# Two reloads moved into a static instruction order, a longer TensorE warm-up, and a new order table

## The chip, the core and the metric

One NeuronCore of a Trainium2 chip runs one program. Its engines each follow an instruction list of their own: PE (TensorE, matrix products), ACT (ScalarE), DVE (VectorE), POOL (GpSimd) and SP (SyncE, which here issues DMA transfers). They meet through semaphores. The metric is the device time of one execution in microseconds (us), and lower is better.

## What is computed

Three stages are chained, all in fp32, the outputs of one being the inputs of the next: landmark attention, a gated MLP, and an MLP with the Mish function.

```python
# q, k, v: (4, 8, 576, 64); m = 32 landmarks
q_lm = q.reshape(B, H, m, S // m, D).mean(axis=3)
k_lm = k.reshape(B, H, m, S // m, D).mean(axis=3)
A, Bm, C = sm(q, k_lm), sm(q_lm, k_lm), sm(q_lm, k)
Z = Bm.transpose(0, 1, 3, 2) / (norm1(Bm) * norminf(Bm) + 1e-06)
for _ in range(6):
    Z = 2 * Z - Z @ Bm @ Z
x = (A @ Z @ C @ v)                # to (2304, 512)
x = (x @ w1) * (x @ w2) @ w3 @ w_out          # 512 -> 1024 -> 1024 -> 512
h = x @ w_in                                  # 512 -> 2048
return (h * np.tanh(softplus(h))) @ w_out2    # 2048 -> 512
```

## The kernel before, in words

**Weights arrive as 64-bit words** and are decoded on the chip, piece by piece, into fp32. A piece `u` takes five steps: `ld u` is the load (SP), `da u` takes the top bits (`top_bits`, L234 on ACT or L236 on DVE), `dm u` the sign (`sign`, L241 on ACT or L243 on DVE), `ds u` rescales (`rescale`, L246, ACT alone) and `db u` joins the halves (`join`, L250, DVE alone). Pieces are named `wo0` to `wo7` (w_out of the gated MLP), `w30` to `w315` (w3), `w000` and up (w1 and w2), and plain numbers (the Mish MLP's w_in and w_out). The raw words lie in a pool of four slots (`raw`) and one of three (`raw2`, tile `raw_74`); a slot is given back when the last step that reads it is issued.

**Matrix products.** w3 and w_out of the gated MLP are multiplied first, in steps `mm n x` (L390, in fp32, each step two matmuls of 128x512). Attention's products of k and q with the landmark means are L564, L485 and L647; the means come from the reductions at L443 (DVE), and copies into block-diagonal tiles at L466 (ACT) and L468 (POOL). The later products are done in three matmuls each, of operands that are split into a high and a low part (`mm3`, L222 to L224): the high part is a copy on ACT (L254), the low part a subtraction on DVE (L259).

**The Mish MLP** goes over three token tiles of 768, and in each over eight quarters of w_in; `g` counts the quarters through all tiles, 0 to 7 in the first, 8 to 15 in the second. A quarter takes seven products by a Strassen scheme, `Z0 g` to `Z6 g` (42 matmuls 128x384), with sums `S`, `Q`, `R`, `C12`, `C21`, `C22` of their results (L1345, DVE, or L1364, ACT), Mish in `E1` to `E3` (L1341 and L1342, ACT), low parts `L1` to `L3` (DVE), and the output products `O0 g` to `O3 g` (36 matmuls 128x512 in all), which run one quarter behind. For a new token tile the tokens' operands are summed and split: `yt`, `yh` (ACT) and `yl` (DVE). While the first tile runs, each split quarter of w_in is stored to DRAM (`zd q`), and each split piece of w_out too (`ws f`), for the later tiles to read back: quarters lie in the two buffers `zw` and `hs`, pieces of w_out in the slots `W_65`, `W_66`, `wy`, `ym` and others.

**What sets the order.** Attention, the gated MLP and the first token tile are cut into named steps. `ORDER` (L29) is one string of step names in a fixed sequence, with an engine behind `@` where a step may run on either of two. `issue()` (L314) walks it and emits each step's instructions, so that an engine's program is the sequence of its own steps in the string. In front of that stand `SPIN` warm-up matmuls on a tile of ones (L1434). Behind it the second and third tile are written out in a loop over `g`; `reload(g)` (L1441) issues the read of the quarter after next and of two pieces of w_out.

```python
    def reload(g):
        if NQ <= g + 2 < NG:
            nc.sync.dma_start(out=f32(zw_all(g)), in_=zd[(g + 2) % NQ])
        for u in (2 * g + 5, 2 * g + 6):
            if 2 * NQ <= u < 2 * NG:
                wo_load(u)

    for g in range(5, NQ):
        reload(g)
    for g in range(NQ, NG):
        ...
```

SP takes its transfers in program order: one whose semaphores are not yet there holds all behind it.

Of the kernel before, what the change touches and what calls it, by code (L numbers as in the profile page):

```python
# [19 lines left out]
SPIN = 20  # L20
# [161 lines left out]
def kernel(  # L182
# [14 lines left out]
    nc = tc.nc  # L197
# [1247 lines left out]
            if 2 * NQ <= u < 2 * NG:  # L1445
                wo_load(u)

    for g in range(5, NQ):
        reload(g)
# [59 lines left out]
```

## Time and profile before

| what | value |
|---|---|
| median of 3 runs | 748.26 us (747.41 to 748.49) |
| the profiled execution | 748.68 us, span 746.9 us |
| busy PE, DVE, ACT, POOL | 720.5, 429.6, 421.0, 16.8 us |
| share of the span | 96%, 58%, 56%, 2% |
| granted TensorE clock, mean | 0.988 of full speed |
| DMA | 141.48 MB, mean 189 GB/s |

The span runs from the profile's first instruction to its last; the time of the execution is a little longer. A clock of 1.00 is 2.4 GHz and 0.50 is 1.2 GHz, the two levels that TensorE's clock has; a value between them is a mean over a stretch.

### The profile page before, as it was taken

How to read it: one execution, taken by the hardware profiler on the slowest of the kernel's cores; microseconds unless marked ns; L12 is line 12 of the kernel's file. 1: busy time of each engine (PE TensorE's matmuls, PEld its weight loads, DVE VectorE, ACT ScalarE, POOL GpSimd, SP SyncE). 2: the span in 40 equal slices, each digit the busy share in tenths (PEclk: the TensorE clock that was granted, in tenths of full speed). 3: DMA queues.
4: the chain of work that ended last, by engine and by line, in shares of the span. 5: the costliest groups of instructions: out<-in, count | busy, mean ns of one | idle time of the engine just before them, and what ended most of it. 6: DMA issues, size and time to landing. Idle time of an engine off the chain costs nothing.

```text
span 746.9 us, 14026 instructions
## 1 busy us (share of the span) xinstructions
PE 720.5 (96%) x5652; PEld 616.6 (83%) x5652; DVE 429.6 (58%) x909; ACT 421.0 (56%) x835; POOL 16.8 (2%) x37
## 2 busy tenths in 40 slices
PE   4999999999999999999999999799999999999997
PEld 1445547888999999999898899688988899889986
DVE  4888768878656746777676777433323463232232
ACT  5897877787858777775665765332222342222222
POOL 0011100100000000000000000000000000000000
PEclk8999999999999999999999999899999999999999
DMA  8877574444325255337456646956445555455502
GB/s 330 295 247 242 172 213 165 122 127 129 117 82 166 90 169 177 135 111 299 190 233 240 239 155 268 387 195 276 154 155 196 215 221 217 167 174 223 195 1 84
DMA packets 48768, 141.48 MB, mean 189 GB/s; under 512 B 3904, under 2 KB 20672, under 8 KB 45120
## 3 DMA queue, kind: packets, MB, share of 16 engines
q1 hardware_dynamic: 48560, 140.46, 52.4%
q8 instruction: 44, 0.72, 0.4%
q14 instruction: 20, 0.16, 0.1%
q10 hardware_dynamic: 144, 0.13, 0.1%
HBM read 110.69 MB, written 29.88 MB: 188 GB/s over the span
## 4 chain that ended last, share of the span: by engine, by line
PE 85%; ACT 7%; DVE 3%; DMA 3%; issue 1%; SPq 0%; DVEq 0%; ACTq 0%
PE ps L222 26%; PE ps L224 25%; PE ps L223 25%; ACT raw L241 3%; PE ps L390 3%; PE ps L883 2%; ACT raw L246 1%; DMA wod<-wy 1%; ACT raw L234 1%; DMA zw<-zd 1%; PE ps L564 1%; PE ps L623 1%; DMA raw<-in_wo_dram 1%; ACT ce L583 1%; PE ps L682 0%
## 5 line engine op out<-in xcount | busy, mean ns | idle before, releaser
L1341 ACT ACTIVATE hsb<-hsb 128x768 f32<-128x768 f32 (+1 forms) x48 | 33.0, 687 | 112.7 <-DVE hsb L1345 112.7
L222 PE MATMUL ps<-hs,W 128*128 128x288 f32 (+1 forms) x298 | 92.6, 311 | 0.0
L223 PE MATMUL ps<-hs,W 128*128 128x288 f32 (+1 forms) x298 | 92.1, 309 | 0.0
L224 PE MATMUL ps<-hs,W 128*128 128x288 f32 (+1 forms) x298 | 92.0, 309 | 0.0
L1345 DVE TENSOR_TENSOR hsb<-ps,zt 128x384 f32<-128x384 f32 x72 | 39.9, 557 | 88.6 <-PE ps L224 88.6
L241 ACT ACTIVATE raw<-raw 128x512 f16<-128x512 f32 x61 | 82.9, 1367 | 8.1 <-DVE raw L236 7.2
L222 PE MATMUL ps<-AT,M 128*128 128x288 f32 x256 | 77.4, 302 | 0.4 <-DVE M L259 0.4
L1345 DVE TENSOR_TENSOR zt<-ps,zt 128x384 f32<-128x384 f32 x48 | 26.7, 557 | 88.8 <-PE ps L224 78.3
L224 PE MATMUL ps<-AT,M 128*128 128x288 f32 x256 | 75.5, 295 | 0.0
L223 PE MATMUL ps<-AT,M 128*128 128x288 f32 x256 | 75.4, 295 | 0.0
L390 PE MATMUL ps<-wo,raw 128*128 128x512 f32 x128 | 62.8, 631 | 11.3 <-DVE wo L250 8.7
L246 ACT ACTIVATE raw<-raw 128x512 f32<-128x512 f32 x88 | 59.2, 677 | 10.6 <-DVE raw L243 9.3
L222 PEld LDWEIGHTS ps<-hs,W 128*128 128x128 f32 x298 | 56.1, 188 | 3.2 <-issue 1.6
L224 PEld LDWEIGHTS ps<-hs,W 128*128 128x128 f32 x298 | 56.2, 189 | 1.7
L223 PEld LDWEIGHTS ps<-hs,W 128*128 128x128 f32 x298 | 56.4, 189 | 1.4
L390 PEld LDWEIGHTS ps<-wo,raw 128*128 128x128 f32 x128 | 24.2, 202 | 36.3 <-issue 20.1
L259 DVE TENSOR_TENSOR W<-hsb,W 128x384 fp32r<-128x384 f32 (+1 forms) x72 | 49.4, 687 | 8.3 <-ACT W L1342 8.3
L222 PEld LDWEIGHTS ps<-AT,M 128*128 128x128 f32 x256 | 48.1, 188 | 3.9 <-issue 1.2
L223 PEld LDWEIGHTS ps<-AT,M 128*128 128x128 f32 x256 | 48.1, 188 | 0.0
L224 PEld LDWEIGHTS ps<-AT,M 128*128 128x128 f32 x256 | 48.1, 188 | 0.0
L1341 ACT ACTIVATE hsb<-ps 128x384 f32<-128x384 f32 x24 | 11.8, 491 | 61.2 <-PE ps L224 61.2
L234 ACT ACTIVATE raw<-raw 128x512 int32<-128x512 uint16 x63 | 42.7, 679 | 1.7 <-DMA raw<-in_wi_dram 1.7
(191 smaller groups left out, 1712.6 us busy)
## 6 DMA issues: line engine op xcount, KB each, us to landing
raw<-in_w_dram SPq DMA_DIRECT2D x64, 256.0 KB, 3.6
zw<-zd SPq DMA_DIRECT2D x8, 1792.0 KB, 7.4
hs<-zd SPq DMA_DIRECT2D x8, 1792.0 KB, 7.1
raw<-in_wo_dram SPq DMA_DIRECT2D x24, 512.0 KB, 4.4
raw<-in_w3T_dram SPq DMA_DIRECT2D x16, 512.0 KB, 4.5
raw<-in_wi_dram SPq DMA_DIRECT2D x16, 512.0 KB, 4.0
zd<-zw SPq DMA_DIRECT2D x4, 1792.0 KB, 7.3
zd<-hs SPq DMA_DIRECT2D x4, 1792.0 KB, 7.8
```

The costliest lines, as they stand in the source:

```text
L222: T.matmul(out=o, lhsT=lh, rhs=rh, start=first, stop=False, skip_group_check=partial)
L223: T.matmul(out=o, lhsT=lh, rhs=rl, start=False, stop=False, skip_group_check=partial)
L224: T.matmul(out=o, lhsT=ll, rhs=rh, start=False, stop=last, skip_group_check=partial)
L234: S.activation(w[..., 0], q[..., 1], ACTF.Copy, scale=2.0 ** -13, bias=2.0 ** -14 - 0.5)
L241: S.activation(w.bitcast(F16)[..., 1], f32(w[..., 1]), ACTF.Copy, scale=2.0 ** -100)
L246: S.activation(f32(w[..., 1]), f32(w[..., 1]), ACTF.Copy, scale=2.0 ** -112)
L259: (G if e == "POOL" else V).tensor_tensor(o, x, f32(hi), op=ALU.subtract)
L390: T.matmul(out=got(f"acc{i}"), lhsT=f32(got(f"w3{n}")[:, o:o + 128, 0]), rhs=WO0[j // 4][:, j % 4], start=j == 0, stop=j == 7)
L564: T.matmul(out=mine(f"cs{g}{hf}")[64 * pr:64 * pr + 64, 0:HALF], lhsT=bdq[:, 2 * g + pr, :], rhs=st["k"][:, 2 * g + pr, hf * HALF:(hf + 1) ...
L883: T.matmul(out=got(f"p{c}{key}")[32 * i:32 * i + 32, 0:256], lhsT=LT[r, b, 2 * c + par, :], rhs=w12(f"w{bp}{s}{c}")[r, par * 256:par * 256 ...
L1341: S.activation(e, src_, ACTF.Mish)
L1345: V.tensor_tensor(o, x, y, op=ALU.add)
```

## The change

The warm-up goes from 20 to 48 matmuls. The reads for the first two quarters of the second tile become steps `rz 0` and `rz 1` of the table, and those of five pieces of w_out become `rw 16` to `rw 20`; the loop that issued them behind the table is taken out. The steps that prepare the second tile's tokens wait for more evictions (`ye`). And the whole of `ORDER` is replaced by another sequence of the same steps (with the seven new ones), with other engines for some: the sign step `dm` stands on ACT 61 times before and 37 times now, on DVE 27 and 51 times; the attention's multiply `amul` stands on POOL 11 times before and 10 now.

```diff
-SPIN = 20
+SPIN = 48
...
-    "ld wo1,da wo1@DVE,dm wo1@ACT,ds wo1,db wo1,ld wo2,da wo2@DVE,dm wo2@ACT,ds wo2,db wo2,ld w30,da w30@ACT,"
+    "ld wo1,da wo1@ACT,dm wo1@ACT,ds wo1,db wo1,ld w30,da w30@ACT,dm w30@DVE,ds w30,ld wo0,da wo0@DVE,dm wo0@DVE,"
...
-    "C21 7,O2 6,yl4 1,E2 7,Z6 7,yh5 1,C12 7,O3 6,L2 7,E3 7,yh6 1,L3 7,yl5 1,yl6 1"
+    "yh6 1,rw 17,yl4 1,yt5 1,yh5 1,yl5 1,yl6 1,rz 1,ws 14,ws 12,rw 19,ws 15,rw 18,rw 20"
...
-            step(name, e, w, fn)
+            step(name, e, w + [f"ye {u} {m}" for u in range(2, 6) for m in range(4)], fn)
+
+    for q in range(2):
+        step(f"rz {q}", "SP", [f"Z{p} {q + 6}" for p in range(7)] + [f"zd {q}", f"zd {q + 6}"],
+             lambda e, q=q: nc.sync.dma_start(out=f32(zw_all(q)), in_=zd[q]))
+    for u in range(16, 21):
+        step(f"rw {u}", "SP", [f"O{p} {(u - 7) // 2}" for p in range(4)] + [f"ws {u - 7}", f"ws {u - 16}"],
+             lambda e, u=u: wo_load(u))
...
-    for g in range(5, NQ):
-        reload(g)
```

The added lines move the line numbers behind them by 5 to 7 (the warm-up from L1435 to L1442, `reload`'s read from L1443 to L1450).

**SP, the end of the table.** These are SP's transfers around the first reloads, before; `wod` and `zd` are the stores in DRAM, so `zd<-zw` writes a quarter and `zw<-zd` reads one.

```order
L1116 DMA zd<-zw_3680 128x3584
L1116 DMA zd<-hs_2122 128x3584
L1078 DMA wod<-ym 128x1024
L1078 DMA wod<-W_65 128x1024
L1078 DMA wod<-wy 128x1024 x2
L1081 DMA wy<-wod 128x1024
L1443 DMA zw_3680<-zd 128x3584
L1081 DMA wy<-wod 128x1024
L1081 DMA ym<-wod 128x1024
L1443 DMA hs_2122<-zd 128x3584
```

The same place now; L1431 is the new read of a quarter.

```order
L1078 DMA wod<-wy 128x1024 x2
L1058 DMA raw<-in_wo_dram 128x1024 x2
L1116 DMA zd<-zw_3733 128x3584
L1078 DMA wod<-ym 128x1024
L1431 DMA zw_3733<-zd 128x3584
L1078 DMA wod<-ym 128x1024
L1116 DMA zd<-hs_2300 128x3584
L1081 DMA wy<-wod 128x1024
L1078 DMA wod<-W_66 128x1024
L1081 DMA wy<-wod 128x1024
L1431 DMA hs_2300<-zd 128x3584
L1078 DMA wod<-ym 128x1024
```

Before, the first read of a quarter (L1443) stood behind the stores of both last quarters (L1116) and of all pieces of w_out (L1078), and behind one read of a piece. Now it stands behind the first of these two stores, and the second, as several pieces' stores, comes after it.

**ACT, the start.** ACT's first steps before, from the first piece on (row by row: sign and rescale of `wo1`, the same of `wo2`, top bits and rescale of `w30` in `raw_74` and of `wo0`, and the three steps of `wo5`).

```order
L241 ACTIVATE raw<-raw 128x512
L246 ACTIVATE raw<-raw 128x512
L241 ACTIVATE raw<-raw 128x512
L246 ACTIVATE raw<-raw 128x512
L234 ACTIVATE raw_74<-raw_74 128x512
L246 ACTIVATE raw_74<-raw_74 128x512
L234 ACTIVATE raw<-raw 128x512
L246 ACTIVATE raw<-raw 128x512
L234 ACTIVATE raw<-raw 128x512
L241 ACTIVATE raw<-raw 128x512
L246 ACTIVATE raw<-raw 128x512
```

And now, where the first four pieces are `wo1`, `w30` (`raw_74`), `wo5` and `wo0`, with `w32` behind them.

```order
L234 ACTIVATE raw<-raw 128x512
L241 ACTIVATE raw<-raw 128x512
L246 ACTIVATE raw<-raw 128x512
L234 ACTIVATE raw_74<-raw_74 128x512
L246 ACTIVATE raw_74<-raw_74 128x512
L234 ACTIVATE raw<-raw 128x512
L241 ACTIVATE raw<-raw 128x512
L246 ACTIVATE raw<-raw 128x512 x2
L234 ACTIVATE raw<-raw 128x512
L241 ACTIVATE raw<-raw 128x512
L246 ACTIVATE raw<-raw 128x512
```

The top bits of the first piece came from DVE and now come from ACT. `wo2` has left the front, and the fourth and last piece that the first products need is rescaled in ACT's eighth and ninth row (printed as one, x2); ahead of it stand two signs as before, and three steps of top bits where there were two.

**DVE, the end of the first tile.** DVE's steps between the last `C12` of the first tile's quarter 7 (the first row) and the second tile's first sum `Q 8` (the last row), before; `sums`, `y` and the `yH`, `yW` tiles are the second tile's tokens.

```order
L1345 TENSOR_TENSOR hsb<-ps_81,zt 128x384
L259 TENSOR_TENSOR W_66<-hsb,W_66 128x768
L259 TENSOR_TENSOR W_66<-hsb,W_66 128x384
L259 TENSOR_TENSOR yH_4177<-sums,yH_4177 128x768
L259 TENSOR_TENSOR yH_4177<-y_3694,ym 128x768
L1345 TENSOR_TENSOR zt<-ps_82,zt 128x384
```

The same place now.

```order
L1345 TENSOR_TENSOR hsb<-ps_79,zt 128x384
L259 TENSOR_TENSOR yH_4067<-sums,yH_4067 128x768
L259 TENSOR_TENSOR ym<-raw,ym 128x512
L259 TENSOR_TENSOR W_66<-hsb,W_66 128x384
L259 TENSOR_TENSOR W_66<-hsb,W_66 128x768
L259 TENSOR_TENSOR yW_4276<-y_3259,yW_4276 128x768
L259 TENSOR_TENSOR yH_3949<-sums,yH_3949 128x768
L1091 TENSOR_TENSOR sums<-y_3259,sums 128x768
L259 TENSOR_TENSOR yH_4263<-sums,yH_4263 128x768
L259 TENSOR_TENSOR yH_4263<-y_3762,ym 128x768
L1345 TENSOR_TENSOR zt<-ps_80,zt 128x384
```

Before, the two low parts of `g` (`W_66<-hsb`) and two low parts of tokens stood there; now there are those, the low part of a piece of w_out (`ym<-raw`), three more low parts of tokens, and the sum `yt5`, which stands right before the low part `yl5` whose high part is made of it.

## Rows read from the trace of the kernel before

**Rows 1.** Stages: length; busy PE, PEld, DVE, ACT, POOL; clock; DMA share; GB/s.
```profile
21.87:48.54 26.67, 23.81 (x440) 13.19 (x441) 21.40 (x52) 24.27 (x44) 2.00 (x7) 1.00 0.84 284
48.54:117.50 68.96, 65.84 (x771) 33.73 (x771) 53.28 (x136) 54.66 (x104) 8.24 (x14) 1.00 0.67 217
117.50:473.50 356.00, 354.81 (x3133) 328.65 (x3123) 249.12 (x553) 253.48 (x538) 4.57 (x6) 1.00 0.48 170
473.50:486.50 13.00, 8.06 (x28) 7.03 (x27) 4.28 (x6) 2.27 (x5) 0.00 (x0) 0.74 1.01 406
486.50:742.80 256.30, 256.30 (x1269) 229.74 (x1267) 89.64 (x150) 72.25 (x129) 0.00 (x0) 1.00 0.47 177
```

**Rows 2.** TensorE's waits over the whole span: us in total, times, longest.
```profile
PE ps L390 <- DVE wo L250: 8.7, 1, 8.7
PE ps L222 <- DMA zw<-zd: 4.9, 1, 4.9
PE ps L390 <- DVE raw L250: 2.5, 3, 1.2
```

**Rows 3.** Timeline of TensorE, start: start us, us, what, idle before and releaser.
```profile
1.45 6.18 PE L1435 MATMUL ps<-ones 128*128 128x512 bf16 x20 [1.45 <-DVE ones L1433]
16.38 5.49 PE L390 MATMUL ps<-wo,raw 128*128 128x512 f32 x6 [8.75 <-DVE wo L250]
21.80 1.25 PE L564 MATMUL ps<-k,bdq 128*64 128x288 f32 x8
```

**Rows 4.** TensorE and clock in single microseconds: length, PE busy, clock, DMA share, GB/s.
```profile
7.00:8.00 1.00, 0.63 (x3) 1.00 0.93 334
12.00:13.00 1.00, 0.00 (x0) 0.50 1.04 400
```

**Rows 5.** Timelines of DVE (first two) and ACT, start.
```profile
5.25 0.74 DVE L236 TENSOR_SCALAR raw<-raw 128x512 uint16<-128x512 uint16 x1 [3.86 <-DMA raw<-in_wo_dram]
16.24 2.60 DVE L443 TENSOR_REDUCE sumq<-q 128x64 f32<-128x1152 f32 x2
10.82 0.65 ACT L246 ACTIVATE raw<-raw 128x512 f32<-128x512 f32 x1
11.38 0.66 ACT L234 ACTIVATE raw<-raw 128x512 int32<-128x512 uint16 x1
12.88 0.65 ACT L246 ACTIVATE raw<-raw 128x512 f32<-128x512 f32 x1 [0.84 <-DVE raw L243]
18.84 0.80 ACT L466 ACTIVATE bdq<-sumq 64x64 f32<-64x64 f32 x3
```

**Rows 6.** Timeline of TensorE where the second token tile begins.
```profile
475.44 0.40 PE L224 MATMUL ps<-W 128*128 128x512 f32 x1
480.77 0.66 PE L222 MATMUL ps<-yW,zw 128*128 128x384 f32 x1 [4.94 <-DMA zw<-zd]
486.03 0.48 PE L222 MATMUL ps<-hs,W 128*128 128x512 f32 x1
```

**Rows 7.** Timeline of SP's queue at the first reload.
```profile
473.12 0.37 SPq L1443 DMA_DIRECT2D zw<-zd  x1
```

**Rows 8.** Groups of instructions by line and form: busy, mean ns, idle before.
```profile
L241 ACT ACTIVATE raw<-raw 128x512 f16<-128x512 f32 x61 | 82.9, 1367 | 8.1 <-DVE raw L236 7.2
L243 DVE TENSOR_SCALAR raw<-raw 128x512 uint16<-128x512 uint16 x27 | 20.1, 754 | 2.5 <-ACT raw L234 2.2
L259 DVE TENSOR_TENSOR W<-hsb,W 128x768 fp32r<-128x768 f32 x24 | 22.8, 952 | 0.0
```

**Rows 9.** Timeline of DVE at the same place as rows 6.
```profile
485.05 0.56 DVE L1345 TENSOR_TENSOR zt<-ps,zt 128x384 f32<-128x384 f32 x1 [7.34 <-issue]
```

**Rows 10.** POOL: the stretched multiply, and the group of its form.
```profile
55.10 1.54 POOL L532 TENSOR_TENSOR e<-e,sm 128x512 f32<-128x512 f32 x1 [6.52 <-ACT raw L246]
L532 POOL TENSOR_TENSOR e<-e,sm 128x512 f32<-128x512 f32 x7 | 7.8, 1118 | 43.8 <-DVE cmx L575 13.1 <-ACT M L254 9.5 <-DVE sm L525 9.4
```

**Rows 11.** DMA issues: KB each, median us from issue to landing.
```profile
raw<-in_w3T_dram SPq DMA_DIRECT2D x16, 512.0 KB, 4.5
```

292 rows, old and new, of the table ORDER are left out of this document.

## The prediction

> **What bounds the kernel now.** I began with the busy time of each engine by stage [rows 1]. From 117.5 us on TensorE (PE) has no slack: 354.81 of 356.00 us, then 256.30 of 256.30 at full clock, with DVE and ACT far below it. In the two early stretches it lacks 2.86 (26.67 - 23.81) and 3.12 us (68.96 - 65.84), 5.98 in all. The stretch 473.5 to 486.5 stands apart: clock 0.74, PE busy 8.06 of 13.00. So the time is PE's matmuls, which the change neither adds to nor takes from (it adds warm-up alone), plus four things: a late start, a slow first few matmuls, 6 us of scattered early waits, and one stall in the middle. PE's own waits name them [rows 2]: 8.7 us for the first weights to be decoded, 4.9 for a reload of the split w_in, 2.5 in three waits for decoded w3. Only after that did I read the places. At the start the 20 warm-ups end at 7.63 (1.45 + 6.18) and the first product starts at 16.38 [rows 3]; by then the granted clock has gone from 1.00 to 0.50 [rows 4], so six matmuls take 5.49 us. At the reload PE's last matmul starts at 475.44, the next at 480.77 after 4.94 us of waiting [rows 6]; the load that it needs was issued at 473.12 [rows 7] and so took 7.5 us, and its issue stood behind a wy load that needed its store to land.
>
> **The change part by part.** The sum is made against the profiled execution, 748.68 us (span 746.9 and 1.8 around it), 0.4 above the median of the runs, 748.26; 0.2% is 1.5 us, and that is about what a measurement of this kernel can tell from no change.
>
> Reload. Before, the first reload of the next tile was issued behind every store of the first tile; now rz 0 needs only Z0 to Z6 of quarter 6 and the stores zd 0 and zd 6, and in SP's queue it stands behind ws 7 and zd 6. Z6 6 is followed on PE by O3 5, the whole of Z 7 and all of O 6, before Z0 8 wants the data: 9 + 42 + 36 = 87 matmuls, and in the last stage 1269 take 256.30 us, 0.202 each [rows 1]: 17.6 us of cover for a load of 7.5, so that it may be issued or land 10 us late. The second, rz 1, is wanted later still, and rw 16 to rw 20 with it. The new waits of the yt, yh and yl steps on the evictions ye are for the end of the gated MLP, some 80 us before them, and cost nothing. The stall of 4.94 goes, and the half clock with it: the matmuls from 480.77 to 486.03 took 5.26 us at clock 0.50 [rows 6], 2.63 at 1.00. Together -7.6. If the cover fails the whole 7.6 comes back.
>
> Start. ACT now does all three decode steps of the first piece. From the landing at 5.25 the steps ahead of the fourth join follow each other, with 0.56 us from one short ACT step to the next (10.82 to 11.38), 1.37 for a sign step on ACT, and 1.50 from the top-bits step to the rescale where DVE does the sign between (11.38 to 12.88) [rows 5, 8]: 5.25 + 0.56 + 1.37 + 0.56 = 7.74 (first piece), + 1.50 + 0.56 = 9.8 (w30), + 0.56 + 1.37 + 2 x 0.56 = 12.9 (wo5, and the rescale of wo0), + about 0.75 for the join = 13.7, against 16.38. The 28 extra warm-ups at 0.21 each (0.63 for 3 [rows 4]) end at 7.63 + 5.9 = 13.5, just before it, so they delay nothing, and the clock is still 1.00: 0.46 a matmul in place of 0.92. Eight matmuls (one step more than before) then end at 17.4. What PE wants next is the product of k with the landmark queries: the two q reductions take 2.60 (16.24 [rows 5]) after the join, to 16.3, then ACT's copies of 0.27 each (0.80 for three) with a top-bits step between them, about 17.4; the second half of k has some 5 MB ahead of and in it behind the first load, 12.5 us at 400 GB/s [rows 4], 17.7. I put the product at 17.9 instead of 21.80: -3.9. Bounds: -2.5 (only the earlier join, the rest taken back by q and k) and -5.4 (both gains in full, 2.7 + 2.7).
>
> Early waits. The sign step stands 61 times on ACT at 1.367 us and 27 times on DVE at 0.754 [rows 8]; the new table has 37 and 51. ACT loses 32.8 us, DVE gains 18.1. Up to the matmuls of the fifth w3 piece (48.54 before) the sums of what each engine has to do ahead of them, rows of the order by these durations, are ACT 35.5 to 30.8 and DVE 31.6 to 32.6. ACT is the fuller in that stretch, 24.27 of 26.67 us [rows 1], so a relief there should take away waits behind rescales: the three for decoded w3 sum to 2.5 [rows 2]. DVE is the next in line, and gets work. Of the 5.98 us I take 2 as gone: most of those three, and something lost behind DVE. Bounds: all 5.98 gone, or 3 more (the first stretch's waits doubled, behind DVE).
>
> DVE at the end of the first tile. Behind the last C12 before stood L2, L3, yl5, yl6; DVE then idled 7.34 us up to the next tile's Q 8 at 485.05 [rows 9], since PE stood still. Now ten steps stand there, and PE no longer waits for it. Let T be the end of Z6 7. PE runs O3 6 (2.0), Z0 8, Z1 8 (1.05 each), O0 7 (2.7), Z2 8 (1.05) and wants bank 1 for Z3 8 at T + 7.9, and that bank is free only after Q 8. DVE: C12 to T + 0.65, yl1 0.87, wl14 0.6, L3 0.5, L2, yl2, yl4, yt5 0.87 each (0.952 for 768 columns less an overlap of 0.08 [rows 8], and by columns for 512 and 384) = T + 6.1; yl5 needs yh5, which ACT can start only when yt5 is done, 0.85 to 0.9: T + 7.0; yl5, yl6, Q 8 = T + 9.4. A new wait of 1.5 us: +1.5. Bounds +0.6 (if yh5 costs nothing) and +2.4.
>
> The rest of the table, 118 to 473 us: PE lacked 1.19 of 356.00 us before [rows 1], ACT and DVE were at 70%, and the move of sign steps leaves both below PE. 0, with up to 2 to lose.
>
> Sum: -7.6 - 3.9 - 2 + 1.5 = -12.0, 748.68 to **736.7 us**.
>
> **Rivals.** (a) DVE takes over early: with the waits kept behind DVE, the start's 3.9 is eaten up to 0.8 by 48 us. For it: DVE has 21.40 of 26.67 us busy there [rows 1] and is now the fuller by the sums (32.6 against 30.8). Against it: DVE idled 5.3 us of that stretch, more than the 1.0 us that it gets. 748.68 - 7.6 - 0.8 + 1.5 = 741.8.
> (b) All early waits go and the start gives 5.4: 748.68 - 7.6 - 5.4 - 6.0 + 0.6 = 730.3. Against it: several of those waits are behind DVE chains of the attention that don't get shorter.
> (c) The reload does not do what it says: rz 0 is held in SP's queue by ws 7 or zd 6, or its 1.8 MB come late among the last loads and stores. It must be 10 us late to stall at all. 748.68 - 3.9 - 2 + 1.5 = 744.3.
> (d) The other side: loads asked for too late. In the new table the raw slot of a weight piece is freed and its matmul wanted with less PE work between for six pieces: 8.4 us for w31, 8.9 for w311, 10.5, 10.8, 11.6 and 11.8 for w310, w315, w010, w314. A load lands in 4.5 us (median [rows 11]) and decoding takes some 3.2, 7.7 together: all six fit. From a landing of about 9.4 us the six lack 4.2, 3.7, 2.1, 1.8, 1.0 and 0.8, 13.6 in all, and the kernel is slower; at 9.5 it is 748.68 - 12.0 + 14.2 = 750.9. Among the loads of the first 20 us this may happen once or twice, not six times.
> (e) POOL's multiplies stretched. The multiply of a 128x512 tile took 1.54 us once, at 55.10, and (7.8 - 1.54) / 6 = 1.05 otherwise [rows 10]; DVE joined two halves of a weight in that moment. Ten multiplies stay on POOL, and DVE has 24 more steps around them. If each lost 0.49 and PE waited for each, +4.9: 741.6. Against it: most of the 5.98 us of early waits are named for decoded weights [rows 2], not for POOL.
> The Trainium skill, page "SBUF — State Buffer", section "Who interferes with whom", speaks for (e): DVE and GpSimd share a port pair under an exclusive lock, and a DVE operation with two SBUF inputs, or in a two-port mode, holds up a GpSimd operation that reads. By that rule moving steps to DVE costs; the one stretched multiply agrees with it, the other six of its size, which ran at their own pace, show how seldom the two meet.
>
> **How the numbers follow.** Forecast 0.47, (a) 0.25, (b) 0.12, (c) 0.07, (d) 0.05, (e) 0.04. The likeliest is 736.7. The low end is (b), 730.3. The high end takes the lower start, the early waits 3 longer and the tail at 2.4: 748.68 - 7.6 - 2.5 + 3.0 + 2.4 = 744.0, which takes in (a), (e) and most mixtures and leaves (c) partly and (d) out. Faster by over 0.2%: all but (d) and a few mixtures of (c) with (a), 0.92; within 0.2% 0.03; slower 0.05.
>
> **What would show it.** In the profile after: the first product at 13.7 with the clock at 1.00 through 20 us; the k product at 17.9; no PE wait for zw<-zd, and the clock at 1.00 all through the middle; a PE wait of 1 to 2 us behind L1345 zt at the first products of the second tile; the waits for decoded raw up to 118 us below 2.5 us in sum. A first product behind 15 us, or waits behind DVE in the first 60 us that sum to over 5, make the forecast wrong towards (a); a wait for raw<-in_w3T loads of several us towards (d); a stall over 1 us at the reload towards (c).

## The result and the profile after

The changed kernel takes 738.6 us (median of 4 runs, 738.44 to 739.11) against 747.84 of the kernel before (its three runs and a fourth): a ratio of 0.9877, 95% interval 0.986 to 0.9894. That is 9.2 us less; 736.7 was forecast, in a range of 730.3 to 744.0. The profiled execution of after took 738.45 us, with a span of 736.5.

TensorE's waits after, over the whole span, answer to [rows 2]:

```profile
PE ps L222 <- DVE hsb L1345: 4.7, 2, 4.0
PE ps L1442 <- DVE ones L1440: 1.5, 1, 1.5
PE ps L647 <- DVE sumk L443: 1.1, 1, 1.1
...
PE ps L222 <- DVE zt L1345: 0.6, 1, 0.6
PE ps L390 <- DVE raw L250: 0.6, 2, 0.3
...
PE ps L222 <- ACT zt L1364: 0.4, 1, 0.4
```

The wait for the reload (4.9) is not there, nor the one for the first weights; the decoded w3 pieces cost 0.6 in place of 2.5. In their place a wait of 4.0 us for a DVE sum stands at the top, which the prediction does not have. The start, on TensorE's timeline, answers to [rows 3]:

```profile
1.45 12.70 PE L1442 MATMUL ps<-ones 128*128 128x512 bf16 x48 [1.45 <-DVE ones L1440]
14.01 3.71 PE L390 MATMUL ps<-wo,raw 128*128 128x512 f32 x8
17.64 1.19 PE L564 MATMUL ps<-k,bdq 128*64 128x288 f32 x8
```

The first product starts at 14.01 (13.7 forecast), right behind the warm-up and at full clock; the k product at 17.64 (17.9 forecast). The stages of after, cut where products start (in the order below: the k product, a product of `sumk` at 48.81, the first split product, the Mish MLP's Z0 0, Z0 8, Z0 9 and Z0 10), have the columns of [rows 1]. The work up to 48.81 is not the same as up to 48.54 before, since the order of the products is another:

```profile
17.64:48.81 31.17, 27.66 (x545) 16.00 (x544) 27.77 (x67) 25.77 (x51) 3.16 (x7) 1.00 0.98 344
48.81:103.00 54.19, 53.91 (x581) 28.34 (x582) 46.05 (x120) 44.13 (x90) 6.98 (x11) 1.00 0.66 211
...
347.62:466.03 118.41, 117.76 (x591) 106.14 (x589) 84.71 (x171) 67.65 (x140) 0.00 (x0) 1.00 0.64 240
466.03:487.40 21.37, 16.34 (x79) 13.79 (x77) 10.32 (x17) 6.52 (x11) 0.00 (x0) 0.99 0.75 260
487.40:504.64 17.24, 17.23 (x79) 15.67 (x80) 6.36 (x11) 4.84 (x10) 0.00 (x0) 0.91 0.63 226
504.64:732.39 227.75, 227.75 (x1128) 204.42 (x1127) 79.15 (x133) 63.20 (x113) 0.00 (x0) 1.00 0.45 174
```

From the k product to 48.81 PE now idles 3.51 us, and from there to 103 it idles 0.28. A quarter of the Mish MLP takes 15.7 us when nothing waits; the first quarter of the second tile took 21.37 and the second 17.24, that one at a clock of 0.91. What held them can be followed back. SP's queue:

```profile
464.14 0.32 SPq L1431 DMA_DIRECT2D hs<-zd  x1
466.23 0.32 SPq L1078 DMA_DIRECT2D wod<-ym  x1
466.60 0.45 SPq L1078 DMA_DIRECT2D wod<-W  x1
476.81 0.32 SPq L1081 DMA_DIRECT2D W<-wod  x1
...
479.61 0.44 SPq L1326 DMA_DIRECT2D out_dram<-hsb  x1
```

The store ws 12 (wod<-W) is issued at 466.60, and rw 19 (W<-wod at 476.81), which overwrites its source, waits for it to land: 9.7 us by SP's list of waits. Behind rw 19 stand the second tile's output stores (L1326), the first at 479.61, although the copy of its block began at 471.27 and took 0.59. The copies use three staging buffers in turn, so the fourth copy, on DVE, waits for the first store:

```profile
486.19 0.69 DVE L1325 COPY hsb<-ps 128x512 f32<-128x512 f32 x1 [7.44 <-DMA out_dram<-hsb]
486.80 0.55 DVE L1345 TENSOR_TENSOR hsb<-ps,zt 128x384 f32<-128x384 f32 x1
```

and the sum C12 8 (L1345) stands behind it in DVE's order, and empties the bank that TensorE wants for Z0 9:

```profile
487.40 0.69 PE L222 MATMUL ps<-yW,hs 128*128 128x384 f32 x1 [4.03 <-DVE hsb L1345]
```

Single stretches of the same place (length, PE busy, clock, DMA share, GB/s) show that the amount of data is at most a part of it: the transfer engines are busy up to 474, but SP waits on until 476.81 while they are nearly idle. The clock falls after TensorE's idle time.

```profile
468.00:470.00 2.00, 2.00 (x11) 1.00 1.16 323
...
472.00:474.00 2.00, 1.36 (x8) 1.00 0.85 341
474.00:476.00 2.00, 2.00 (x11) 1.00 0.08 31
476.00:478.00 2.00, 2.00 (x13) 1.00 0.22 31
...
488.00:489.00 1.00, 1.00 (x5) 0.50 1.00 377
```

So the account between the two profiled executions, by the start of the named product:

| first matmul of | before | after | gained by then |
|---|---|---|---|
| k product | 21.80 | 17.64 | 4.2 |
| Z0 0 (Mish MLP) | 357.25 | 347.62 | 9.6 |
| Z0 8 (second tile) | 480.77 | 466.03 | 14.7 |
| Z0 10 | 514.65 | 504.64 | 10.0 |
| last | 742.41 | 732.39 | 10.0 |

The account reads: 9.6 us come from the part up to the first tile and 5.1 from the reload's wait; then 4.7 are given back in two quarters. These take 38.6 us against 33.9 before, and the 33.9 held the half clock behind the reload. The rest of the 10.4 us of span lies behind the last product.

### The profile page after: what moved, and what is told of

Read it like the earlier page. It is cut to its first block, busy times and chain, and to the rows that moved or that the text cites. A ratio compares the mean times of both kernels' runs of the same rounds, so it can differ in the third digit from the quotient of the medians.

```text
span 736.5 us, 14067 instructions
## 1 busy us (share of the span) xinstructions
PE 721.4 (98%) x5680; PEld 618.0 (84%) x5680; DVE 444.0 (60%) x933; ACT 393.2 (53%) x813; POOL 16.5 (2%) x35
## 4 chain that ended last, share of the span: by engine, by line
PE 87%; DVE 5%; DMA 4%; ACT 2%; issue 1%; SPq 0%; DVEq 0%; ACTq 0%
PE ps L222 26%; PE ps L224 26%; PE ps L223 26%; PE ps L390 4%; DMA k<-in_kT_dram 2%; PE ps L883 2%; DMA out_dram<-hsb 1%; PE ps L682 1%; PE ps L623 1%; PE ps L564 1%; DVE sumk L443 1%; DVE raw L250 1%; DVE sumq L443 1%; DMA raw<-in_wo_dram 1%; PE ps L542 1%
## 5 line engine op out<-in xcount | busy, mean ns | idle before, releaser
L1341 ACT ACTIVATE hsb<-hsb 128x384 f32<-128x384 f32 (+1 forms) x48 | 32.8, 683 | 111.6 <-DVE hsb L1345 111.6
L1345 DVE TENSOR_TENSOR hsb<-ps,zt 128x384 f32<-128x384 f32 x72 | 39.9, 557 | 86.5 <-PE ps L224 86.5
L1345 DVE TENSOR_TENSOR zt<-ps,zt 128x384 f32<-128x384 f32 x48 | 26.7, 557 | 82.7 <-PE ps L224 80.1
L390 PE MATMUL ps<-wo,raw 128*128 128x512 f32 x128 | 59.6, 603 | 0.6 <-DVE raw L250 0.6
L241 ACT ACTIVATE raw<-raw 128x512 f16<-128x512 f32 x37 | 50.3, 1359 | 0.5
```

What stands on the lines that cost most here:

```text
L241: S.activation(w.bitcast(F16)[..., 1], f32(w[..., 1]), ACTF.Copy, scale=2.0 ** -100)
L390: T.matmul(out=got(f"acc{i}"), lhsT=f32(got(f"w3{n}")[:, o:o + 128, 0]), rhs=WO0[j // 4][:, j % 4], start=j == 0, stop=j == 7)
L1341: S.activation(e, src_, ACTF.Mish)
L1345: V.tensor_tensor(o, x, y, op=ALU.add)
```

## Experiments

Theory 1, from this profile: **SP's queue**. The moved reads are hidden, but those of w_out (rw 18 to rw 20) stand ahead of the output stores, one of them waits for a store, and the output stores, the staging buffers, DVE's next sum and TensorE follow. Theory 2: the transfer engines are full, and the stores are late wherever they stand. Theory 3: DVE's longer list at the end of the first tile.

**The reads of w_out behind the third output store** (changed kernel; the diff leaves out that rw 18, rw 19 and rw 20 go out of the table's last line):

```diff
-    for u in range(16, 21):
+    for u in range(16, 18):
...
+            if name == "O1 7":
+                for u in (18, 19, 20):
+                    wo_load(u)
```

> The changed kernel with rw 18 to rw 20 issued behind the third output store of the second tile instead of ahead of all output stores. Theory 1 (SP's queue): the 4.03 us wait of TensorE at 487.4 comes from the output stores, which stand in SP's queue behind rw 19, and rw 19 waits 9.7 us for the store ws 12 to land; with the stores ahead of it that wait and the half clock behind it (about 1.3) go: 738.6 - 5.3 = 733.3 us, first output store at 473 or earlier. Theory 2 (full transfer rings): the stores would land late wherever they are issued, since the read of a quarter and the last stores share the 16 DMA engines; then 2 us or more of the wait stay: 735.5 to 738.6. Theory 3 (DVE's longer list at the tile's end): nothing changes, 738.6.

734.2 us (732.99 to 736.99), ratio to the kernel before 0.9824 (0.9804 to 0.9845). SP's queue there:

```profile
467.55 0.32 SPq L1078 DMA_DIRECT2D wod<-ym  x1
467.92 0.43 SPq L1078 DMA_DIRECT2D wod<-W  x1
468.44 0.41 SPq L1078 DMA_DIRECT2D wod<-hs  x1
473.21 5.21 SPq L1326 DMA_DIRECT2D out_dram<-hsb  x3
```

The same three stores of w_out are under way, and the one that rw 19 waited for lands no sooner to speak of (9.2 us after its issue, 10.2 in after). The output stores, though, now go out from 473.21 on, and TensorE has no wait at Z0 9: from Z0 8 to Z0 10 it takes 32.9 us in place of 38.6. Theory 1 holds. Theory 2 falls, and so does theory 3 as the cause by itself, since DVE's list is the same here.

**DVE's end of the first tile in another order** (changed kernel, the order string alone):

```diff
-    "...,zd 7,C12 7,yh4 1,yl1 1,wl 14@DVE,rw 16,E3 7,L3 7,L2 7,yh2 1,ws 13,yl2 1,"
-    "yh6 1,rw 17,yl4 1,yt5 1,yh5 1,yl5 1,yl6 1,rz 1,..."
+    "...,zd 7,yl1 1,wl 14@DVE,C12 7,yh4 1,yt5 1,rw 16,E3 7,L2 7,L3 7,yh2 1,ws 13,yh5 1,"
+    "yl4 1,yh6 1,rw 17,yl2 1,yl5 1,yl6 1,rz 1,..."
```

> The changed kernel with DVE's steps at the end of the first tile put in another order: yl1 and wl 14 ahead of C12 7, where DVE idles, yt5 right behind it, and yh5 well ahead of yl5. The waits of TensorE on zt there (0.37 and 0.64) should go by all theories. Theory 1 (SP's queue): the later wait for the output stores grows by what is saved, since the stores' time is set by ws 12 on SP: 738.5 us, no change. Theory 3 (DVE's list sets the wait at 487): 1 to 6 us less, 732.5 to 737.6.

736.32 us (733.66 to 737.44; the profiled execution is the fastest), ratio 0.9838 (0.9818 to 0.9857). The time lies in the range that I had given for theory 3. The waits on zt are gone, and the wait at Z0 9 is 3.09, not longer. What theory 1 had left out: in the changed kernel ws 14 stands ahead of ws 12 in SP's queue, and its low part wl 14 comes from this very list on DVE; SP waited 1.7 us for it. With wl 14 earlier, ws 12 is issued 1.05 us ahead of Z0 8 and not 0.57 behind. So DVE's list matters here, but by this trace through SP's queue.

```profile
483.85 0.45 PE L222 MATMUL ps<-yW,hs 128*128 128x384 f32 x1 [3.09 <-DVE hsb L1345]
```

**Both edits together.**

> The changed kernel with both edits: rw 18 to rw 20 behind the third output store, and DVE's steps at the tile's end in the new order. Theory 1: both waits go, 738.6 - 5.3 - 1.2 = 732.1 us. If the first edit leaves part of the wait (theory 2): 734 to 737.

734.57 us (730.53 to 735.71), ratio 0.9799 (0.9773 to 0.9824). Z0 8 to Z0 9 takes 15.67 and Z0 9 to Z0 10 15.68 us: nothing waits there any more. The median is not below the first edit's and lies in the range that I had given for theory 2. By the trace this is not its doing but a matter of what lies ahead: this profiled execution reached Z0 0 at 350.91, the one of after at 347.62, with the same order up to there. I come back to that spread.

**The reads behind the table again** (changed kernel without the steps rz and rw, with the loop of before):

> The changed kernel without the steps rz and rw: the reads stand behind the table again, as before the change, in the new order and with the long warm-up. The stall at the first reload returns. Theory 1: it covers the waits on zt and the late output stores, so the net is only the difference of the two stalls, and since ws 13 to ws 15 are ahead of the read it lands at about 475 for a product that is wanted at 466, 9 us of waiting and 2.6 of half clock against 6.3 saved: 744 us. If the two stalls are independent of each other: 738.6 + 11.6 = 750 us. If moving the reads was worth nothing in this order: 738.6.

746.08 us (744.78 to 750.71), ratio 0.998 (0.9965 to 0.9995): 7.5 more than the changed kernel. TensorE waits 12.07 us for zw<-zd, and neither for zt nor for the output stores, which start late behind the stall anyway. So the one stall hides the other, as theory 1 has it; the time lies between the 744 that I had given for this and the 750 of two independent stalls.

```profile
478.11 0.66 PE L222 MATMUL ps<-yW,zw 128*128 128x384 f32 x1 [12.07 <-DMA zw<-zd]
```

**The seven steps alone** in the kernel before (rz 0 behind zd 6, the others at the end of its table):

> The kernel before with the steps rz and rw alone: rz 0 right behind zd 6, the others at the table's end. If the reload's term is as predicted, -7.6: the read is issued when zd 6 has landed, near 465, lands near 473, and is wanted at 475.8, no stall: 740.7. Theory 1 (SP's queue) also asks what comes later: the output stores stand behind rw 16 to rw 20, which wait for ws 9 and ws 10 (about 476), so the stores start at 478 to 480, and the fourth output copy is wanted near 487: at most 2 us of new waiting, 740.7 to 742.7. Rival: a wait of the same kind and size as in the changed kernel (5.3 us) appears here too: 746.

751.96 us (749.07 to 754.1), ratio 1.004 (1.0028 to 1.0053): slower than before. The reload's wait is gone and the other kind is longer. Its SP queue and TensorE's wait:

```profile
466.43 1.00 SPq L1078 DMA_DIRECT2D wod<-wy  x2
481.60 1.60 SPq L1081 DMA_DIRECT2D wy<-wod  x2
...
486.01 1.61 SPq L1326 DMA_DIRECT2D out_dram<-hsb  x3
...
500.23 0.69 PE L222 MATMUL ps<-yW,hs 128*128 128x384 f32 x1 [8.90 <-DVE hsb L1345]
```

rw 16 waits some 14 us for the last two stores; I had reckoned with 2 us of new waiting on TensorE at most. Here the transfer engines do have a part: from 470 to 480 their share is 0.84 to 1.04, and the two stores land 15.5 us after their issue, against 8.8 in the kernel before. So the load sets how long rw 16 waits; whether TensorE pays for it is the next run's question.

**The same with the reads of w_out behind the output stores**: rz 0 and rz 1 in the table, and in the loop `for u in {"O0 7": (16, 17), "O1 7": (18, 19, 20)}.get(name, ()): wo_load(u)`.

> The kernel before with rz 0 and rz 1 in the table, and the five reads of pieces of w_out behind the second and third output store of the second tile instead of ahead of all output stores. If the moved reads are worth the 4.94 us stall and 2.6 us of half clock, and only the output stores behind them took that back in the run with all seven steps: 748.5 - 7.6 = 740.9 us, the second tile's first product about 5 us earlier and no long wait at the ninth quarter. If something else in that place stands in the way: 745 to 752.

740.68 us (740.23 to 741.08), ratio 0.99 (0.9877 to 0.9922). This is 7.7 less than the 748.35 of before. The same two stores land as late as in the run above (15.6 us), yet the stretch that had the stall [rows 1] runs full and at full clock:

```profile
473.50:486.50 13.00, 13.00 (x67) 11.75 (x66) 6.81 (x11) 4.36 (x9) 0.00 (x0) 1.00 1.01 395
```

The three runs together show the price of the reload (7.6 forecast, 7.7 measured) and that it is had only where the output stores keep their place.

**20 warm-ups in the changed kernel, and 48 in the one before.**

> The changed kernel with 20 warm-up matmuls in place of 48. If the clock at the first products was worth what the prediction has for it: the clock falls to 0.50 at about 12 us, the eight matmuls take 7.3 us in place of 3.7, the k product starts at 21.2 in place of 17.64, and 2.5 to 3.6 us are lost for good: 741.1 to 742.2. Rival: q and k are late anyway, and a wait behind them (1.08 us for sumk) and DVE take most of it up: 738.6 to 739.7.

> The kernel before with 48 warm-up matmuls alone. The first product stays at 16.38 (the decoding is as before), the warm-ups end at 13.7, and the clock, which fell about 4 us after the last warm-up before, is still at or near 1.00 when the first product starts: six matmuls in 2.7 in place of 5.49 us. If nothing takes that up: 748.3 - 2.7 = 745.6. Rival: DVE's decoding and the k and q reductions set what comes next, so that the next waits grow by as much: 747.5 to 748.3.

With 20 in the changed kernel: 737.8 us (736.3 to 738.09), ratio 0.9859 (0.9845 to 0.9872), no slower than with 48 and below both of my cases. With 48 in the kernel before: 747.85 (746.73 to 748.27), ratio 0.9989 (0.998 to 0.9998), which is 0.6 us less and not 2.7. In its trace the k product starts 2.6 us earlier (19.21) and Z0 0 only 0.6 (356.69). In the run with 20, TensorE's start is

```profile
13.92 6.21 PE L390 MATMUL ps<-wo,raw 128*128 128x512 f32 x8 [6.07 <-DVE wo L250]
20.06 1.19 PE L564 MATMUL ps<-k,bdq 128*64 128x288 f32 x8
```

so the clock is half there for the most part (it is back at 1.00 from 19 us), and the k product is 2.4 us later than in after; 3.6 was reckoned. But Z0 0 starts at 348.04 (347.62 in after). From the k product to 49 us PE idles 0.71 here and 3.51 in after: DVE and the k loads set the pace. In after the chain of work that ended last runs there over a load of k and DVE's reduction of it, not over the first products:

```profile
8.82 9.66 DMA k<-in_kT_dram
18.50 1.35 DVE sumk L443
```

Because the output stores might have hidden the rest, the fastest version was run with 20 too:

> The changed kernel with both edits (loads behind the third output store, DVE's steps at the tile's end) and 20 warm-up matmuls in place of 48. If the long warm-up has a lasting worth that the late output stores hid: 2.4 us slower than with 48, 737.0. If the start's gain is used up before the first split product, as the anchors of the run with 20 say (0.4 us at the first product of the Mish MLP): 734.0 to 735.2.

731.48 us (730.53 to 731.71), ratio 0.9774 (0.9755 to 0.9793): no slower than the 0.9799 of the same kernel with 48, and below both of my cases. Its median is the lowest here. Nothing in these runs shows a lasting worth of the long warm-up in the new order.

**The engines of the sign steps.** The new order with the old engines, the old order with the new ones (44 steps swapped in each), and the new order with the old engines for w_out and w3 alone (7 steps):

> The changed kernel with every sign step on the engine that it had before the change (44 steps: 34 back to ACT, 10 back to DVE), in the new order. The early part gained 4.6 us beyond the start. If the relief of ACT made that: 2 to 4.6 us are lost again, 740.6 to 743.2. If the order of the steps and loads made it: 737.6 to 739.6. Later stretches have room on both engines and should not move.

> The kernel before, its order kept, with every sign step on the engine that it has after the change (44 steps: 34 from ACT to DVE, 10 the other way). If the relief of ACT alone makes the early gain of 9.6 us: 4 to 9 us less, 739.5 to 744.5. If engines and order only work together: 747 to 755, as the changed kernel with the old engines was 15 us slower.

> The changed kernel with only the sign steps of w_out and w3 (the first 118 us) on the engines of before: 5 back to ACT, 2 to DVE. With all 44 swapped the first split product was 6 us late, the 400th 13.4 us. If these few steps made the first 6: 744 to 745, less what the late output stores absorb. If the pieces of w1 and w2 behind them made nearly all: 738 to 740.

753.45 us (748.97 to 757.03), ratio 1.0064 (1.0044 to 1.0083); 752.41 (750.84 to 753.21), ratio 1.0053 (1.0035 to 1.007); 742.82 (741.64 to 743.76), ratio 0.9927 (0.9904 to 0.995). Z0 0 starts at 363.21, 360.07 and 350.48, against 347.62 in after and 357.25 in before. The first case loses 6.1 us up to the first split product, another 7.3 up to the 400th, and 2.2 from there to Z0 0. The second shows that the engines by themselves gain nothing: in the old order they cost 2.8 us at Z0 0. Order and engines gain only together. I had expected the first at 740.6 to 743.2 and was far off; the third lies between my two cases.

## Why the prediction was right, point by point

**Direction and range** held, and the reload's term is the one that the runs confirm best: -7.6, measured -7.7 by itself. That the total came so near is in part luck: a cost of some 5.6 us that the sum left out and an early gain that it put 3.7 us too low go opposite ways.

**The step that failed** is the sentence that costs the other moved reads at nothing ("The second, rz 1, is wanted later still, and rw 16 to rw 20 with it"). It asked when their data are wanted and not what stands behind them in SP's queue. One of these reads held SP for 9.7 us with the output stores behind it, and the kernel loses 4.03 us of waiting and 1.6 of half clock (17.24 against 15.68 from Z0 9 to Z0 10). Rival (c) looked for a hold in that queue ahead of the read, not behind it.

**The start** came as forecast at the k product (17.64, 17.9), but what the warm-up has in its -3.9 is no lasting gain: 20 in place of 48 moved the changed kernel by -0.8 us, and 48 in place of 20 the one before by -0.6. **The early waits** were undersized: start and early part together were to give 5.9, and gave 9.6 at Z0 0, of which 2.4 is the earlier first product, 2.7 the six cold matmuls (5.42 us from 16.38 to 21.80, at half the clock), and 2.2 idle time of PE up to the Mish MLP (6.4 before, by [rows 1] with the 0.45 up to the 400th product, and 3.51 + 0.28 + 0.46 after). The remaining 2.3 is in no wait that the view names; it lies in PE's busy time, which from the k product to Z0 0 sums to 329.0 us before and 325.7 after, with two matmuls (0.9) fewer. Why the same matmuls take less there is open. That the whole 9.6 needs order and engines jointly is shown by the two swaps; which steps of the order make it is not. That the warm-up's share of it can be had without the warm-up does not contradict this: with 20 PE idles less later.

**Rival (a)** had DVE eat the start's gain up to 0.8 by 48 us. DVE is indeed the fuller engine now (27.77 of 31.17 us, ACT 25.77), but the gain stayed: from the first product to 49 us TensorE has done 31.5 us of products, and by the same time before 27.1, with the six cold ones counted at half of their time. **Rival (d)** did not come: no wait of TensorE for a load of w3 is in the list, and ACT's for them up to 118 us sum to 1.9, against 4.8 before. **Rival (e)** did not come as it was put: the seven multiplies of the large size average 1050 ns, so none was stretched, with 24 more sign steps on DVE. But the two engines did meet, and DVE was held. Two joins that began with 1.02 and 0.49 us of a multiply still to run took 1.58 and 1.04 us, where a join otherwise takes about 0.69. In [rows 10] the join had begun first, at 55.03, and the multiply was the longer one. These rows agree with the exclusive lock of the Trainium skill ("SBUF — State Buffer", "Who interferes with whom"). TensorE did not pay for it: it idles 0.46 us in all from 103 to Z0 0.

```profile
L532 POOL TENSOR_TENSOR e<-e,sm 128x512 f32<-128x512 f32 x7 | 7.3, 1050 | 53.9 <-DVE sm L525 30.1 <-DVE py L739 14.2 <-ACT et L611 9.6
...
141.40 1.05 POOL L532 TENSOR_TENSOR e<-e,sm 128x512 f32<-128x512 f32 x1 [0.82 <-DVE sm L525]
141.43 1.58 DVE L250 SCALAR_TENSOR_TENSOR w<-raw 128x512 int32<-128x512 int32 x1
```

**DVE at the end of the first tile** was right in mechanism: Q 8 ended at 473.32, 9.2 us after the end of Z6 7 (9.4 forecast), with the idle time of 0.91 for yh5 ahead of yl5. The new wait was 0.64, and 0.37 for an ACT copy that stands behind yh5: 1.0 against 1.5.

## What to carry to other kernels

When a transfer is moved forward in a queue that is served in order, ask what stands behind it as well as what it needs: a read that waits for a store holds every later store, and a staging buffer hands that on to the engines. Measure the part that is moved by itself, with and without its neighbours: here it was worth 7.7 us by itself, and with five harmless-looking reads beside it the kernel was 3.5 us slower than before. A gain at the start is a gain only if it is still there at a later mark; compare the start of the same product in both traces.

## What was not expected of the hardware

A store of 512 KB, issued just behind a read of 1.8 MB, took 10 us to land (wod<-W, 466.60 to 476.8) although the transfer engines, busy until 474, were at a share of 0.08 from 474 to 476. What the last microseconds of it were is open.

The same order of steps reached Z0 0 at 346.53 to 350.91 us in five profiled executions with 48 warm-ups (after, the two edits apart and together, the reads put back). The runs of the changed kernel lie closer together (738.44 to 739.11) than those of the first edit (732.99 to 736.99). This may be luck, or the stall takes up what the early part gains and loses; that is not settled.

After a wait of 2.90 us (20 warm-ups) and of 4.03 (after) the clock was 0.50 for the matmuls that followed, after 3.09 (DVE's new order) it stayed at 1.00.
